# The scale of the exponentials from a ScalarE register in place of a per-partition operand

## The chip, the core and the metric

The kernel runs on one core of a Trainium2 chip. The core's engines have a queue each and run side by side: TensorE (PE in the profile; its weight loads are PEld), VectorE (DVE), ScalarE (ACT), GpSimd (POOL), and SyncE (SP), which here issues all the DMAs. The metric is the device time of the program in microseconds. The time before is 1566.49 us, the median of three runs (1566.06 to 1568.72).

## The reference

A transformer block whose attention and feed-forward parts both read the same normalised input (2048 rows of 512, 32 heads of 16, hidden width 1792, all float32):

```python
xn = _layernorm(x, axis=-1)
return x + _A_ref(xn, A_wqkv, A_wo) + _B_ref(xn, B_w1, B_b1, B_w2, B_b2)

# _A_ref, for 32 heads:
scores = jnp.einsum("bhqd,bhkd->bhqk", q, k) * (Dh ** -0.5)
p = _softmax(scores, axis=-1)
o = jnp.einsum("bhqk,bhkd->bhqd", p, v)
return (lambda x, *d: x.transpose(*d))(o, 0, 2, 1, 3).reshape(B, S, D) @ wo

# _B_ref:
h = jnp.einsum("bsd,df->bsf", x, w1) + b1
h = _gelu(h)                 # the tanh form
return jnp.einsum("bsf,fd->bsd", h, w2) + b2
```

## The kernel before

All matmuls of q, k, scores, output and feed-forward run on pairs of float16 halves (a high part and what is left), with weights scaled by powers of two. So the scores in PSUM are too large or small by a factor, which the softmax's exponential takes out: `sexp`, a tile of 128 partitions by 4 columns, holds that factor times 1/4, one column for each weight block of 128 columns, that is for two groups of four heads. All 128 partitions of a column hold the same value. DVE writes a column when it prepares that weight block (L463, L464), long before the first exponential that reads it, but for column 0.

Attention runs in units. There are 8 groups of four heads and 4 blocks of 512 queries, so 32 pairs; a pair has 16 units, 512 in all. In one unit, for each of four heads:

- `s_half` (L238 on) multiplies 128 queries by 512 keys into a PSUM bank `pS`, and DVE reduces it to row maxima, `mt` (L250). After 16 units the maxima of the pair are known, are negated (`mneg`, L261), split (`mhl`, L271 and L272) and written by DMA into two more rows of the query stack, so that the next product subtracts them.
- `e_half` (L284 on), 20 units later, multiplies 128 keys by 512 queries into a bank `pT`, and ACT takes the exponential of it into an SBUF tile `pe` (L295), with `scale=sexp[:, g // 2:g // 2 + 1]`. This is the instruction that the change touches; there are 2048 of it.
- `v_half` (L298 on), one or two units later, multiplies the exponentials by the values and a column of ones into `pV`; after 16 units ACT copies it out (`osb`, L321).

`unit` (L589 on) writes these in a fixed order: two score products, two exponential products, the value products on one half of TensorE's rows and, on the other half, some products of a filler (`pD`). The filler is first the projection of the next heads (ACT copies `pf`, L497), then the feed-forward part: DVE takes its hidden rows out of PSUM (`hh`, L996), GpSimd and ACT make the gelu (ACT's tanh, L963), and ACT takes out the sums (`yt`, L1022). TensorE's order is the written order (all queues are written out by hand, `ORDERED`), and most of its tiled products have one helper line, L169.

There are eight PSUM banks. The `pS` products turn through three, the `pT` products through three; one is the filler's `pD` (it and the `pT` banks change places when a filler group ends), and one holds `pV`. So a `pT` product waits until the exponential three before it has read its bank, and a `pS` product until the reduction three before it has. `given(engine, ns)` (L159) adds an estimate to a counter, which `unit` lowers; nothing reads it to set the order.

Of the kernel before, what the change touches and what calls it, by code (L numbers as in the profile page):

```python
# [10 lines left out]
I32 = mybir.dt.int32  # L11
AF = mybir.ActivationFunctionType
# [35 lines left out]
def layer_kernel(ctx: ExitStack, tc: tile.TileContext, x, wqkv, wo, w1, b1, w2, b2, out):  # L48
    nc = tc.nc
# [45 lines left out]
    sexp = const.tile([P, 4], F32, name="sexp")  # L95
# [11 lines left out]
    def banks(tag):  # L107
        k = free_banks[tag].pop(0)
        free_banks[tag].append(k)
        return bank_tile(k, tag)  # L110
# [48 lines left out]
    def given(engine, ns):  # L159
        backlog[engine] += ns  # L160
# [34 lines left out]
    def tiled(user, dst, lhs, rhs, start, stop):  # L195

        for j in range(0, P, 32):
            product(user, dst[j:j + 32], lhs[:, j:j + 32], rhs, start=start, stop=stop)


    mt_of, ptiles, pv_of = {}, {}, {}
    queue, slot = [], [0]

# [80 lines left out]
    def e_half(u, n):  # L284

        p, a = divmod(n, 2)
        t, kt = divmod(u, 16)
        g, qb = divmod(t, NQB)
        st = banks("T")
        r = slice(64 * a, 64 * a + 64)  # L290
        k0 = (kt % 4) * P
        tiled(None, st, kst[g % 2][p][kt // 4][r, k0:k0 + P], qst[g % 2][p][qb][r, :], True, True)
        pe = work.tile([P, QB], F32, name="pe", bufs=12)
        ptiles[u, n] = pe
        nc.scalar.activation(pe, st, AF.Exp, scale=sexp[:, g // 2:g // 2 + 1])  # L295
        given("act", 580)

    def v_half(u, a):  # L298

# [289 lines left out]
    def unit(gen):  # L589
# [7 lines left out]
        for a in range(2):  # L597
            for b in range(2 * a, 2 * a + 2):
                if u < NU:
                    s_half(u, b)  # L600
                if 0 <= e < NU:
                    e_half(e, b ^ 1)
            if e >= 0:
                enter()

                w, r = (e - 2, 1) if a == 0 else (e - 1, 0)
                live = 0 <= w < NU
                new = r == 0 and w % 16 == 0
                if live and not new:
                    v_half(w, r)  # L610
                dense(gen, 1 - r)
                if live and new:
                    v_half(w, r)

                for user, goes_on in (("V", live and not (r == 1 and w % 16 == 15)),
                                      ("D", cur[0] is not None and not cur[0].over())):
                    leave(user, goes_on)
                for k in backlog:
                    backlog[k] = max(0, backlog[k] - HALF)
                if live and r == 1:  # L620
                    v_end(w)
                ended()
# [559 lines left out]
```

## Time and profile before

| | us |
|---|---|
| median of the timed runs | 1566.49 |
| lowest and highest of them | 1566.06, 1568.72 |
| span of the profiled execution | 1563.9 |
| PE busy | 1521.8 |
| DVE busy | 1432.4 |
| ACT busy | 1376.1 |
| first and last exponential start | 128.4, 1530.9 |

The span goes from the first to the last instruction of one profiled execution; its own time is not listed beside it, so the timed median stands for it, 2.6 us above the span. A line such as L295 names an instruction of the kernel above. In a group of instructions, the count is followed by the busy time in us, the mean ns of one, the idle time of its engine just before them, and what ended that idle time. Busy times of one engine are unions, so overlapping neighbours are counted once. Ends of matmuls are modelled, and a few matmul records are missing. The granted clock of TensorE was 0.994 of full speed over the span.

### The profile page before, as it was taken

Reading aid. Unit: us, or ns where it says so; the run is one execution under the profiler, and the core shown is the slowest. Engines: PE = TensorE matmul, PEld = TensorE weight load, DVE = VectorE, ACT = ScalarE, POOL = GpSimd, SP = SyncE. Lnnn points to the kernel's source line nnn. Section 1 sums busy time; section 2 is a strip of 40 time slices with the busy share of each in tenths; the row PEclk is TensorE's granted clock in tenths of the full one; section 3 lists DMA queues with packets and bytes.
Section 4 is the critical chain, followed back from the end, with each engine's and each line's share of the span. In section 5 each row is a group of like instructions: output and inputs, shape, how many; then the busy total and the mean of one; then the engine's idle time right before and its main releaser. Section 6 shows DMA issues by size and latency. Waiting matters only on the chain.

```text
span 1563.9 us, 86366 instructions
## 1 busy us (share of the span) xinstructions
PE 1521.8 (97%) x39203; PEld 810.0 (52%) x39203; DVE 1432.4 (92%) x2428; ACT 1376.1 (88%) x2270; POOL 673.1 (43%) x694
## 2 busy tenths in 40 slices
PE   8999999999999999999999999999999999999997
PEld 4434555555555555555555555555555555555443
DVE  7889989999999999999999999999999999999612
ACT  4317999999999999999999999999999999999881
POOL 3113697446454444435443443654343454521000
PEclk9999999999999999999999999999999999999997
DMA  6454576442201211131122111121112111021512
GB/s 201 128 158 141 175 231 217 155 124 75 62 23 53 83 36 32 34 81 35 35 55 65 45 35 35 38 75 56 35 42 63 42 34 35 21 66 57 156 45 85
DMA packets 113672, 123.73 MB, mean 79 GB/s; under 512 B 24988, under 2 KB 85276, under 8 KB 113304
## 3 DMA queue, kind: packets, MB, share of 16 engines
q1 hardware_dynamic: 113304, 118.21, 25.6%
q8 instruction: 306, 5.01, 1.3%
q14 instruction: 62, 0.51, 0.1%
HBM read 80.61 MB, written 37.34 MB: 75 GB/s over the span
## 4 chain that ended last, share of the span: by engine, by line
PE 79%; DVE 14%; ACT 2%; DMA 2%; issue 2%; SPq 1%; POOL 0%; ACTq 0%; DVEq 0%; POOLq 0%
PE pV L169 23%; PE pS L169 19%; PE pD L169 18%; PE pT L169 15%; DVE mt L250 9%; DVE hh L996 3%; ACT pe L295 1%; PE pT L430 1%; PE pS L430 1%; DVE amx L658 1%; PE pT L523 1%; PE pD L430 1%; DMA ac<-acc_d 0%; PE pV L523 0%; SPq L1055 0%
## 5 line engine op out<-in xcount | busy, mean ns | idle before, releaser
L295 ACT ACTIVATE pe<-pT,sexp 128x512 f32<-128x512 f32 x2048 | 1267.7, 688 | 68.2 <-PE pS L169 21.3
L250 DVE TENSOR_REDUCE mt<-pS 128x1 f32<-128x512 f32 x2048 | 1291.7, 683 | 38.1 <-PE pS L169 20.3
L169 PE MATMUL pV<-pe,vv 64*32 64x512 f32 x8192 | 1076.6, 595 | 0.2
L169 PE MATMUL pT<-qst,kst 64*32 64x512 f16 x8192 | 712.8, 378 | 2.3 <-ACT pe L295 2.1
L169 PE MATMUL pS<-kst,qst 62*32 62x512 f16 x8192 | 638.8, 379 | 20.9 <-DVE mt L250 17.8
L169 PEld LDWEIGHTS <-qst 62*32 62x32 f16 x8192 | 277.3, 91 | 268.4 <-issue 114.4
L169 PEld LDWEIGHTS <-kst 64*32 64x32 f16 x8192 | 282.2, 91 | 177.0 <-issue 77.2
L169 PE MATMUL pD<-xb,wc 64*32 64x512 f16 x5376 | 370.5, 377 | 0.0
L169 PE MATMUL pD<-w_s,g 64*32 64x512 f16 x5376 | 359.4, 377 | 0.0
L169 PEld LDWEIGHTS pV<-pe,vv 64*32 64x32 f32 x8192 | 182.3, 105 | 106.3 <-PE pV L169 16.9
L974 POOL TENSOR_TENSOR t<-hh 128x512 f32<-128x512 f32 x56 | 58.2, 1039 | 350.0 <-DVE hh L996 350.0
L169 PEld LDWEIGHTS <-g 64*32 64x32 f16 x5376 | 115.1, 92 | 40.8 <-issue 0.4
L169 PEld LDWEIGHTS <-wc 64*32 64x32 f16 x5376 | 114.0, 91 | 35.9 <-issue 0.4
L169 PE MATMUL pD<-xt,wqk_h 64*32 64x512 f16 x1920 | 127.2, 378 | 1.7 <-issue 1.6
L351 POOL TENSOR_TENSOR osb<-osb,rb 128x512 f32<-128x512 f32 x31 | 39.8, 1285 | 131.6 <-DMA rb<-den_d 131.6
L1024 POOL TENSOR_TENSOR xa<-xa,yt 128x512 f32<-128x512 f32 x32 | 40.9, 1279 | 117.1 <-ACT yt L1022 117.1
L1061 DVE SCALAR_TENSOR_TENSOR ac<-pS,gs,ac 128x512 f32<-128x512 f32 x20 | 15.0, 751 | 67.2 <-PE pT L169 46.9
L969 POOL TENSOR_TENSOR t<-t,hh 128x512 f32<-128x512 f32 x56 | 71.6, 1279 | 4.7
L976 POOL TENSOR_TENSOR t<-t,hh 128x512 f32<-128x512 f32 x56 | 71.6, 1279 | 4.7
L971 POOL TENSOR_TENSOR g<-t,g 128x512 f16<-128x512 f32 x56 | 65.2, 1164 | 4.7
L968 POOL TENSOR_SCALAR t<-t,gs 128x512 f32<-128x512 f32 x56 | 38.8, 692 | 57.6 <-ACT t L963 57.6
L169 PE MATMUL pS<-wo_s,oc 64*32 64x512 f16 x1008 | 61.7, 378 | 0.3
(139 smaller groups left out, 880.5 us busy)
## 6 DMA issues: line engine op xcount, KB each, us to landing
wch<-in_B_w_dram SPq DMA_DIRECT2D x28, 512.0 KB
wc<-w_d SPq DMA_DIRECT2D x56, 256.0 KB
qk_d<-stg SPq DMA_DIRECT2D x32, 256.0 KB
rb<-den_d SPq DMA_DIRECT2D x124, 64.0 KB
w_d<-wsp SPq DMA_DIRECT2D x28, 256.0 KB
kst<-qk_d SPq DMA_DIRECT2D x128, 48.0 KB
qst<-qk_d SPq DMA_DIRECT2D x128, 48.0 KB
xs<-in_A_x_dram SPq DMA_DIRECT2D x16, 256.0 KB
```

The source lines that it names most:

```text
L169: p = nc.tensor.matmul(*args, **kw)
L250: nc.vector.reduce_max(mt_of[t][:, n, qt, kb:kb + 1], s, axis=AX.X)
L295: nc.scalar.activation(pe, st, AF.Exp, scale=sexp[:, g // 2:g // 2 + 1])
L351: pooled((1280, lambda: nc.gpsimd.tensor_tensor(osb, osb, rb, op=ALU.mult)), (620, lambda: nc.gpsimd.tensor_scalar(ot[:, 0], osb, 1.0, 0.0 ...
L430: nc.tensor.matmul(self.bank, lhs, rhs, start=start, stop=self.last and self.over())
L968: pooled((690, lambda: nc.gpsimd.tensor_scalar(t1, t1, 1.0, gs[:, 1:2], op0=ALU.add, op1=ALU.mult)), (1280, lambda: nc.gpsimd.tensor_tenso ...
L969: (1280, lambda: nc.gpsimd.tensor_tensor(t1, t1, hh, op=ALU.mult)),
L971: (1160, lambda: nc.gpsimd.tensor_tensor(g[:, 1, f, :], t1, g[:, 0, f, :], op=ALU.subtract)),
L974: pooled((1040, lambda: nc.gpsimd.tensor_tensor(t1, hh, hh, op=ALU.mult)), (620, lambda: nc.gpsimd.tensor_scalar(t1, t1, 1.0, 1.0 / GELU_A ...
L976: (1280, lambda: nc.gpsimd.tensor_tensor(t1, t1, hh, op=ALU.mult)),
L996: nc.vector.tensor_scalar(hh, hp, scale, bias, op0=ALU.mult, op1=ALU.add)
L1024: add = lambda: nc.gpsimd.tensor_tensor(xa, xa, yt, op=ALU.add)
```

## The change

The exponentials' scale is no longer an operand of 128 values in SBUF but a register of ScalarE. `exp_scale(m)` loads the register from partition 0 of column `m` of `sexp`, when `m` is another than the one it holds; since `m` is the group's number halved, that happens four times. The estimate of the exponential's time, 580 ns, becomes 470.

```diff
+    scale_reg, held = nc.scalar.alloc_register("exp_scale"), [None]
+
+    def exp_scale(m):
+
+        if held[0] != m:
+            nc.scalar.reg_load(scale_reg, sexp[0:1, m:m + 1].bitcast(I32))
+            held[0] = m
+        return scale_reg
+
     mt_of, ptiles, pv_of = {}, {}, {}
     queue, slot = [], [0]
...
-        nc.scalar.activation(pe, st, AF.Exp, scale=sexp[:, g // 2:g // 2 + 1])
-        given("act", 580)
+        nc.scalar.activation(pe, st, AF.Exp, scale=exp_scale(g // 2))
+        given("act", 470)
```

New lines shift those below: L295 before is L304 in the changed kernel, L1022 is L1031, L963 is L972. On ScalarE the first load stands ahead of the table load and the first exponentials, behind the copies of the projection. After the change:

```order
L506 ACTIVATE pf<-pT 128x512 x3
L506 ACTIVATE pf<-pD 128x512
L206 TENSOR_LOAD sexp
L304 ACT_TABLE_LOAD
L304 ACTIVATE pe<-pT 128x512 x4
```

One row is new there, and the exponentials no longer name `sexp`. The second load stands where the third group of four heads begins, between two sets of four exponentials. Before (a tanh, then eight exponentials, a copy `yt`, two more, and the copy `osb`):

```order
L963 ACTIVATE t_13381<-t_13381 128x512
L295 ACTIVATE pe<-pT,sexp 128x512 x8
L1022 ACTIVATE yt<-pD,gs 128x512
L295 ACTIVATE pe<-pT,sexp 128x512 x2
L321 ACTIVATE osb<-pV 128x512
```

After:

```order
L972 ACTIVATE t_13382<-t_13382 128x512
L304 ACTIVATE pe<-pT 128x512 x4
L206 TENSOR_LOAD sexp
L304 ACTIVATE pe<-pT 128x512 x4
L1031 ACTIVATE yt<-pD,gs 128x512
L304 ACTIVATE pe<-pT 128x512 x2
L330 ACTIVATE osb<-pV 128x512
```

The third and fourth load stand in the same way at the fifth and seventh group. On all other engines the rows and their order are the same but for the line numbers.

## Prediction

> **What bounds the kernel now.** I read the busy shares and the chain of waits on the page first.
>
> ```profile
> PE 1521.8 (97%) x39203; PEld 810.0 (52%) x39203; DVE 1432.4 (92%) x2428; ACT 1376.1 (88%) x2270; POOL 673.1 (43%) x694
> PE 79%; DVE 14%; ACT 2%; DMA 2%; issue 2%; SPq 1%; POOL 0%; ACTq 0%; DVEq 0%; POOLq 0%
> ```
>
> ACT, whose instructions the change makes cheaper, has 2% of the chain. Taken alone this says that the change is worth nothing. The shares are averages over stages, so the next view is the table of stretches, with the attention loop (first exponentials to the last score products) in one stretch:
>
> ```profile
> 180.49:1436.72 1256.23, 1239.02 (x34400) 678.52 (x34403) 1222.81 (x2022) 1200.99 (x1982) 612.41 (x603) 1.00 0.23 66
> 400.00:1400.00 1000.00, 988.02 (x27419) 541.21 (x27410) 980.52 (x1622) 958.16 (x1582) 452.58 (x456) 1.00 0.17 46
> 656.00:664.00 8.00, 8.00 (x248) 4.42 (x248) 7.92 (x14) 7.55 (x13) 4.37 (x5) 1.00 0.02 5
> 664.00:672.00 8.00, 7.84 (x220) 4.46 (x205) 7.41 (x12) 8.00 (x15) 4.27 (x5) 1.00 0.33 86
> ```
>
> The columns are PE, weight loads, DVE, ACT and POOL, busy us and instruction count. Three engines are nearly full: in the 1000 us from 400 on, PE is idle 12.0, DVE 19.5 and ACT 41.8 us. So none has room for long, and each can hold the others for a moment. The last two rows show such a moment. From 664 to 672 ACT is busy for all of the 8.00 us; PE starts 220 matmuls against 248 in the 8 us before, although it is called busy for 7.84 us; DVE falls from 7.92 to 7.41 us. PE's busy time does not tell its pace. What ACT did there:
>
> ```profile
> 665.10 0.60 ACT L321 ACTIVATE osb<-pV 128x512 f32<-128x512 f32 x1
> 665.58 1.28 ACT L295 ACTIVATE pe<-pT,sexp 128x512 f32<-128x512 f32 x2
> 666.72 0.66 ACT L963 ACTIVATE t<-t 128x512 f32<-128x512 f32 x1
> 667.24 2.45 ACT L295 ACTIVATE pe<-pT,sexp 128x512 f32<-128x512 f32 x4
> 669.51 0.75 ACT L1022 ACTIVATE yt<-pD,gs 128x512 f32<-128x512 f32 x1
> 670.09 3.14 ACT L295 ACTIVATE pe<-pT,sexp 128x512 f32<-128x512 f32 x5
> 669.56 2.56 DVE L250 TENSOR_REDUCE mt<-pS 128x1 f32<-128x512 f32 x4 [0.42 <-PE pS L169]
> ```
>
> Three instructions that are no exponentials come within 4.4 us, ACT runs without a gap, and DVE then waits 0.42 us for a score product. PE takes its instructions in order: a pT product that waits for a pT bank, which an exponential has not yet read out, holds the pS products behind it, for which DVE waits. This is where ACT sets the end: not in the plain units, but for a unit or two after each extra instruction.
>
> **The price of the operand.** The groups of ACT by form:
>
> ```profile
> L295 ACT ACTIVATE pe<-pT,sexp 128x512 f32<-128x512 f32 x2048 | 1267.7, 688 | 68.2 <-PE pS L169 21.3 <-PE pT L169 19.1 <-ACT pe L295 0.2
> L963 ACT ACTIVATE t<-t 128x512 f32<-128x512 f32 x56 | 35.6, 636 | 0.0
> L1022 ACT ACTIVATE yt<-pD,gs 128x512 f32<-128x512 f32 x32 | 22.2, 695 | 0.0
> L497 ACT ACTIVATE pf<-pD 128x512 f32<-128x512 f32 x21 | 12.6, 598 | 6.0 <-PE pS L126 3.6 <-PE pD L169 1.5 <-PE pS L169 0.5
> L713 ACT ACTIVATE xs<-xs,sd 128x512 f32<-128x512 f32 x6 | 4.0, 714 | 0.2
> ```
>
> L1022 and L497 are the same copy from PSUM, with and without a scale that is read from a tile: 695 against 598 ns, 97 ns. The exponential, 688 ns, reads such a scale too (sexp among its names). L963 multiplies by a constant scale and reads no scale tile: 636 ns from SBUF, against 714 for L713, which reads one: 78 ns. So the cost is the reading of the operand and not the multiplication. I take 97, from the pair that reads PSUM like the exponential does: it becomes 591 ns. What counts is the distance between starts, since neighbours overlap. In the rows above, four exponentials in a row take 2.45 us, so they start (2.45 - 0.69)/3 = 0.587 us apart; after L321, which reads no operand, the next starts 665.58 - 665.10 = 0.48 us later. So the distance falls by 0.10 us, to about 0.49. In the loop that is 1848 exponentials times 0.10 = 185 us of ACT's time.
>
> ```profile
> L295 ACT ACTIVATE pe<-pT,sexp 128x512 f32<-128x512 f32 x1848 | 1143.0, 688 | 53.1 <-PE pS L169 19.0 <-PE pT L169 8.9 <-ACT pe L295 0.2
> L250 DVE TENSOR_REDUCE mt<-pS 128x1 f32<-128x512 f32 x1848 | 1165.6, 683 | 30.7 <-PE pS L169 14.0 <-PE pT L169 3.9 <-PE pD L169 1.3
> ```
>
> Nearly all of it becomes idle time. 1848/4 = 462 units in 1256.23 us make 2.72 us for a unit of four exponentials. They need 4 x 0.587 = 2.35 us now and 4 x 0.49 = 1.96 us then. An extra instruction of about 0.5 us now overruns its unit by 2.35 + 0.5 - 2.72 = 0.13 us and takes the next unit's room as well; then it fits into its own unit with 0.26 us left.
>
> **What of it reaches the end.** DVE's reductions stay as they are, and no matmul is removed. So the gain is at most the time in which DVE waits in this loop: 1256.23 - 1222.81 = 33.4 us. The part that can go is where its reductions wait for PE for long enough to be named, by the view of waits for 400 to 1400, and then for 180 to 400:
>
> ```profile
> DVE mt L250 <- PE pS L169: 8.2, 31, 0.4
> DVE mt L250 <- PE pT L169: 0.9, 4, 0.3
> ...
> DVE mt L250 <- PE pS L169: 5.1, 10, 1.5
> DVE mt L250 <- PE pT L169: 3.0, 8, 0.6
> ```
>
> The 9.1 us of the first stretch I count as gone: 35 waits of 0.26 us on average, the size of a unit's overrun and of the one shown at 669.56. The other gaps before the reductions there are short ones in plain units, where the products themselves come late; they stay. Of the 8.1 us of 180 to 400 I count half, 4: up to 1.5 us long, they also have loads and weight preparation behind them, and no row divides them. Before 180 and after 1437 I count nothing: the first exponentials come at 128, and in the tail there are no reductions and ACT is busy 119.00 of 136.00 us:
>
> ```profile
> 1400.00:1536.00 136.00, 134.74 (x3587) 69.10 (x3580) 78.52 (x130) 119.00 (x194) 12.99 (x12) 1.00 0.27 83
> ```
>
> Gain: 9.1 + 4 = 13.1 us, bounds 0 and 33.4.
>
> **The four loads.** Each stands in ACT's own queue, ahead of an exponential: one ahead of the table load and the first exponential, three at the change of head pairs in mid-loop. They wait only for a sexp value that DVE wrote one quarter of the heads earlier, so for nothing. Behind each stand the exponentials, and behind those PE's next pT product. The trace has no register load. The nearest rows of ACT are
>
> ```profile
> L295 ACTq EVENT_SEMAPHORE  x509: 17/17/1093, 137.0 to 1529.0; - x170
> L295 ACT ACT_TABLE_LOAD  x1: 1283/1283/1283, 127.1 to 127.1; - x1
> ```
>
> 17 ns for a queue instruction that finds its value there, 1283 ns for one that brings in state. I take the middle, 0.65 us, for want of a nearer row, and let all four reach the end: 2.6 us, bounds 0.1 and 5.1. If a unit's slack hid them, the result would be 2.6 us better.
>
> The Trainium skill, "DMA: Bandwidth & Descriptors", section "Latency and other measured facts", puts the floor of a tensor load at about 600 ns; by it the four would cost 2.4 us and the sum below would be 0.2 us lower. No run here shows it yet.
>
> The estimate at L304 (470 for 580) only adds to a counter that nothing reads for the order. All other engines keep their rows, so it costs nothing and needs no cover.
>
> **Sum.** Against the profiled span: 1563.9 - 13.1 + 2.6 = 1553.4 us. The timed median, 1566.49, lies 2.6 us above that span; I keep this distance: 1556 us.
>
> **The rivals.**
> *PE is the bound after all.* For it: PE's 79% of the chain, and that PE names waits for exponentials for only 2.1 us in all:
>
> ```profile
> PE pT L169 <- ACT pe L295: 2.1, 7, 0.7
> ```
>
> Then 2.1 us are gained and 2.6 paid: 1567 us. Against it stand 220 matmuls against 248 in equal busy time. The Trainium skill, "Perfetto Trace Analysis", section "Identifying the Most-Contended Engine", says that matmul busy time is a poor measure of how near PE is to its limit, and to look at weight-load busy time. By that rule PE, with 52% of weight loads, would have room; the trace agrees as far as the matmul counts go.
>
> *All of DVE's waiting goes.* DVE then runs without a gap: 1566.5 - 33.4 + 2.6 = 1536 us. For it: ACT would be idle some 20% of the loop. Against: the plain units wait for products too.
>
> *The register does not count as a constant.* The exponential stays at 688 ns: only the loads are left, 1566.5 + 2.6 = 1569 us. Against it speaks L963, whose scale costs nothing; but its constant stands in the instruction, and a register is not seen anywhere in this trace.
>
> *Slower: the register is fetched at each instruction, and neighbours no longer overlap.* Exponentials would start 0.688 us apart. With the loop's other ACT work, 1200.99 - 1143.0 = 58 us, ACT would need 1848 x 0.688 + 58 = 1329 us for a loop of 1256: 73 us more, 1642 us with the loads. It decides from a distance of (1256 - 58)/1848 = 0.648 us on, 0.06 above today's. For it: each of the 1848 would need the register. Against: no row shows that ACT's queue is late; it names only PE as what its idle exponentials wait for.
>
> **How the numbers follow.** The forecast has 0.65, PE as bound 0.13, all of DVE's waiting 0.11, an unchanged exponential 0.06, lost overlap 0.05. The range for 8 in 10 goes from 1543 (a gain of 26 us of the 33.4, loads nearly free) to 1567 (PE as bound). A measurement of this kernel tells about 0.2%, 3.1 us, from no change; faster than 1563.4 are the forecast and the full gain, and none of the others: 0.76. Within 0.2% falls PE as bound, with a part of the unchanged exponential: 0.15. Slower: 0.09.
>
> **What would show it.** Exponentials of 585 to 600 ns, about 0.49 us apart in the rows of x4; L1022 unchanged at 695. ACT's busy time in the loop down by about 185 us, to some 81% of it. The named waits of DVE's reductions from 400 to 1400 down from 9.1 to under 2 us, DVE over 99% busy there. Gaps of 0.1 to 1.3 us on ACT at the four loads. I am wrong in the step on what reaches the end if the exponentials shrink and the span does not; in the price if they stay at 688; in the loads if the gaps there reach several us.

## The result and the profile after

The changed kernel takes 1558.35 us, the median of 7 runs (1554.96 to 1560.89); before it is 1566.49 us in 7 runs of the same comparison (1563.89 to 1571.85). The ratio is 0.9942, with a 95% interval of 0.9927 to 0.9958: 0.58% faster, some 9 us of 1566. The medians alone lie 8.1 us apart. The profiled span goes from 1563.9 to 1557.1 us.

The page of the changed kernel, with the busy shares and the chain:

```profile
PE 1513.2 (97%) x39203; PEld 808.8 (52%) x39203; DVE 1429.9 (92%) x2428; ACT 1221.3 (78%) x2270; POOL 674.7 (43%) x694
PE 80%; DVE 15%; issue 2%; DMA 1%; SPq 1%; ACT 0%; POOL 0%; DVEq 0%; ACTq 0%; POOLq 0%
```

ACT lost 154.8 us of busy time and the span lost 6.8. ACT's 2% of the chain are gone. Its groups by form, and the exponentials' neighbours:

```profile
L304 ACT ACTIVATE pe<-pT 128x512 f32<-128x512 f32 x2048 | 1109.8, 597 | 208.8 <-PE pS L169 99.3 <-PE pT L169 79.2
L1031 ACT ACTIVATE yt<-pD,gs 128x512 f32<-128x512 f32 x32 | 22.0, 688 | 3.6 <-PE pT L169 0.3 <-PE pS L169 0.2
```

An exponential takes 597 ns instead of 688, as long as the copies without an operand (593 to 605). The other forms stay: the copy with an operand is at 688 ns for 695, tanh at 636 for 636. ACT's idle time before exponentials rises from 68.2 to 208.8 us: the shorter exponentials mostly wait longer for their products. The stretches of the loop, in the columns of the table before:

```profile
180.49:1430.00 1249.51, 1229.56 (x34344) 676.17 (x34336) 1218.77 (x2018) 1059.82 (x1976) 611.54 (x601) 1.00 0.23 66
400.00:1400.00 1000.00, 988.54 (x27616) 544.24 (x27612) 986.29 (x1633) 855.77 (x1595) 455.37 (x458) 1.00 0.17 47
```

From 400 to 1400 DVE is now busy for 986.29 us instead of 980.52, and does 1633 instructions instead of 1622. ACT has 144 us to spare. What DVE's reductions still wait for there, and the group with all its idle time:

```profile
DVE mt L259 <- PE pS L169: 3.5, 18, 0.5
...
L259 DVE TENSOR_REDUCE mt<-pS 128x1 f32<-128x512 f32 x1492 | 939.0, 682 | 11.7 <-PE pS L169 3.5
```

The named waits fell from 9.1 to 3.5 us, the whole idle time before the reductions from 17.4 to 11.7 us, and 1492 reductions fit into the 1000 us instead of 1481, 0.74% more.

The same copy, tanh and four exponentials that stood without a gap before stand like this now:

```profile
663.28 1.08 ACT L304 ACTIVATE pe<-pT 128x512 f32<-128x512 f32 x2 [0.29 <-PE pT L169]
664.25 0.60 ACT L330 ACTIVATE osb<-pV 128x512 f32<-128x512 f32 x1
664.74 1.09 ACT L304 ACTIVATE pe<-pT 128x512 f32<-128x512 f32 x2
665.70 0.65 ACT L972 ACTIVATE t<-t 128x512 f32<-128x512 f32 x1
666.22 2.09 ACT L304 ACTIVATE pe<-pT 128x512 f32<-128x512 f32 x4
653.08 15.35 DVE L259 TENSOR_REDUCE mt<-pS 128x1 f32<-128x512 f32 x24
```

ACT waits 0.29 us for a product before the two exponentials ahead of the copy, so it comes to the extra instructions with nothing left over. DVE runs 24 reductions in a row, to 668.43, without a named wait.

The four loads are in the trace too (first the view of their line, then ACT's rows around the second, at 487.6):

```profile
L206 ACTq TENSOR_LOAD <-sexp x4: 274/280/887, 125.1 to 1174.9; - x4
...
486.27 2.19 ACT L304 ACTIVATE pe<-pT 128x512 f32<-128x512 f32 x4
```

The three loads in the loop take 274 to 283 ns. The second falls inside a set of four exponentials: it starts 0.24 us after the third of them, and the fourth starts 0.49 us after the third, the usual distance. The load goes on in the queue while the exponential ahead of it is still under way.

### The profile page after: what moved, and what is told of

Same layout as the page of the kernel before. It is cut to its first block, busy times and chain, and to the rows that moved or that the text cites. A ratio compares the mean times of both kernels' runs of the same rounds, so it can differ in the third digit from the quotient of the medians.

```text
span 1557.1 us, 86371 instructions
## 1 busy us (share of the span) xinstructions
PE 1513.2 (97%) x39203; PEld 808.8 (52%) x39203; DVE 1429.9 (92%) x2428; ACT 1221.3 (78%) x2270; POOL 674.7 (43%) x694
## 4 chain that ended last, share of the span: by engine, by line
PE 80%; DVE 15%; issue 2%; DMA 1%; SPq 1%; ACT 0%; POOL 0%; DVEq 0%; ACTq 0%; POOLq 0%
PE pV L169 24%; PE pS L169 19%; PE pD L169 18%; PE pT L169 15%; DVE mt L259 10%; DVE hh L1005 3%; PE pT L439 1%; PE pS L439 1%; DVE amx L667 1%; PE pT L532 1%; PE pV L532 0%; SPq L1064 0%; DMA ac<-acc_d 0%; PE pD L439 0%; DMA qk_d<-stg 0%
## 5 line engine op out<-in xcount | busy, mean ns | idle before, releaser
L304 ACT ACTIVATE pe<-pT 128x512 f32<-128x512 f32 x2048 | 1109.8, 597 | 208.8 <-PE pS L169 99.3
L169 PEld LDWEIGHTS <-qst 62*32 62x32 f16 x8192 | 280.9, 91 | 268.9 <-issue 112.0
L169 PEld LDWEIGHTS <-kst 64*32 64x32 f16 x8192 | 267.0, 91 | 166.4 <-issue 68.0
```

Of the source, the lines that this page charges most:

```text
L169: p = nc.tensor.matmul(*args, **kw)
L304: nc.scalar.activation(pe, st, AF.Exp, scale=exp_scale(g // 2))
```

## The experiments

The ratio is against the kernel before, timed beside each of them (its medians there are 1565.62 to 1566.82 us). The last column is a number that startup differences do not touch: the time from the start of the 257th to that of the 1793rd exponential (384 units) in the profiled execution. It comes from one execution each. Kernels that should agree in it do so within 0.5 us: 1038.4 and 1038.9 with the operand, 1030.7 to 1030.9 with a register or a constant. Below, "in the loop" means this number.

| kernel | median us | ratio and 95% interval | 257th to 1793rd, us |
|---|---|---|---|
| before | 1566.49 | 1 | 1038.4 |
| changed (register) | 1558.35 | 0.9942 (0.9927 to 0.9958) | 1030.8 |
| const_scale | 1556.91 | 0.9937 (0.9923 to 0.9950) | 1030.9 |
| loads_only | 1567.14 | 1.0005 (0.9993 to 1.0016) | 1038.9 |
| half_register | 1559.32 | 0.9952 (0.9938 to 0.9965) | 1032.6 |
| load_each_unit | 1557.78 | 0.9939 (0.9925 to 0.9953) | 1030.7 |
| operand_no_tanh | 1564.42 | 0.9982 (0.9972 to 0.9991) | 1035.7 |
| register_no_tanh | 1558.70 | 0.9954 (0.9938 to 0.9970) | 1031.8 |
| register_hh_act | 1556.48 | 0.9938 (0.9925 to 0.9951) | 1027.8 |
| operand_hh_act | 1573.00 | 1.0036 (1.0022 to 1.0051) | 1043.9 |
| register_late_bank | 1577.96 | 1.0067 (1.0048 to 1.0086) | 1042.9 |
| register_mid_bank | 1559.99 | 0.9956 (0.9940 to 0.9972) | 1031.6 |
| reg_late_bank_hh_act | 1596.56 | 1.0192 (1.0172 to 1.0211) | 1063.1 |
| two_operands | 1624.05 | 1.0369 (1.0350 to 1.0387) | 1088.5 |

### The register and the loads by themselves

A constant in place of the register:

```diff
-        nc.scalar.activation(pe, st, AF.Exp, scale=exp_scale(g // 2))
+        nc.scalar.activation(pe, st, AF.Exp, scale=2.0 ** -8)
```

> The scale is the constant 2^-8 written into the instruction (the value that these inputs give for every head; the four loads are gone). Theory (a register costs an exponential nothing more than a constant, and the four loads are hidden): exponentials of 597 ns as with the register, and the time within 2 us of the register form, 1556 to 1560 us. Rival (the register still costs something at each instruction, or the loads reach the end with the 2.6 us of the prediction): 2.5 us or more faster than the register form, under 1556 us.

Measured: 1556.91 us, 1.4 us under the register form, with intervals that overlap; in the loop 1030.9 against 1030.8 us. Its exponentials are as long as with the register:

```profile
L304 ACT ACTIVATE pe<-pT 128x512 f32<-128x512 f32 x2048 | 1109.8, 597 | 206.1 <-PE pS L169 109.4 <-PE pT L169 76.6
```

A register costs no more than a constant that could be measured here, and the four loads, which this run lacks, do not show either.

The loads without their use:

```diff
-        nc.scalar.activation(pe, st, AF.Exp, scale=exp_scale(g // 2))
+        exp_scale(g // 2)
+        nc.scalar.activation(pe, st, AF.Exp, scale=sexp[:, g // 2:g // 2 + 1])
```

> The four register loads stay, but the exponentials take their scale from the tile again. Theory (a load of 0.28 us runs beside the exponential that is already under way): same as before, 1565 to 1568 us, exponentials 688 ns. Rival (each load reaches the end): with the 0.65 us of the prediction each, 2.6 us slower, 1569 us.

Measured: 1567.14 us, the same as before. But the trace has no load: at its line it shows four waits of 17 ns, presumably because nothing reads the register. So this run says only that the four waits are free. The loads themselves are tried by loading the register for each unit:

```diff
-        if held[0] != m:
+        if held[0] != u:
...
-        nc.scalar.activation(pe, st, AF.Exp, scale=exp_scale(g // 2))
+        nc.scalar.activation(pe, st, AF.Exp, scale=exp_scale(u, g // 2))
```

> The register is loaded anew for each unit, 512 loads in place of 4. Theory (a load is hidden behind the exponential under way or the wait for the next product): within 3 us of the register form, 1557 to 1561 us. Rival (a load holds up ACT's queue for its whole 0.28 us, and that is no longer free when it comes in each unit): ACT needs 4 x 0.49 + 0.28 = 2.24 us of a unit, so still less than before, but an extra instruction overruns again: 1561 to 1566 us. If each load reached the end in full: 512 x 0.28 = 143 us more, 1700 us.

Measured: 1557.78 us, and 1030.7 us in the loop. 512 loads cost no more than 4:

```profile
L206 ACTq TENSOR_LOAD <-sexp x512: 272/277/1386, 127.9 to 1519.4; - x171
```

The loads take 154 us together and none of it appears. In the trace all 512 begin while an ACT instruction is still under way, and 505 of them end beside one too; the other seven end in ACT's wait for the next product.

### How much of the shortening is needed

Half of the exponentials with the register, half with the operand:

```diff
-        nc.scalar.activation(pe, st, AF.Exp, scale=exp_scale(g // 2))
+        nc.scalar.activation(pe, st, AF.Exp, scale=exp_scale(g // 2) if n < 2 else sexp[:, g // 2:g // 2 + 1])
```

> Two of the four exponentials of a unit take the register, two the tile. ACT needs 2 x 0.49 + 2 x 0.587 = 2.15 us of a unit of 2.72, so an extra instruction of 0.5 us still fits into its own unit. Theory A (the gain is that an extra instruction no longer overruns its unit, and is used up once it fits): three quarters or more of the gain, 1558 to 1560.5 us. Theory B (every exponential that frees its bank sooner gives its own share): half of the gain, about 1562.5 us.

Measured: 0.9952 against 0.9942; in the loop 5.8 of 7.6 us, three quarters of the gain for half of the shortening. That is theory A's number. The intervals of the two ratios overlap, and half of the gain (0.9971) lies outside this one's, 0.9938 to 0.9965.

The edit in the other direction, a second operand for each exponential in the kernel before:

```diff
+    zero = const.tile([P, 1], F32, name="zero")
+    nc.gpsimd.memset(zero, 0.0)
...
-        nc.scalar.activation(pe, st, AF.Exp, scale=sexp[:, g // 2:g // 2 + 1])
+        nc.scalar.activation(pe, st, AF.Exp, scale=sexp[:, g // 2:g // 2 + 1], bias=zero)
```

> The kernel before with a second operand per partition on each exponential, a bias tile of zeros: the edit in the other direction. By 0.10 us for an operand the distance between exponentials goes from 0.587 to 0.69 us. Theory (ACT's load against a unit's room has a knee: free below, in full above): ACT needs 1848 x 0.69 + 58 = 1333 us for a loop of 1256, so 60 to 100 us slower than before, 1625 to 1665 us. Rival (the time goes with the exponential's duration evenly, 9 us for 0.09 us): 9 us slower, 1575 us. Second rival (a bias tile costs nothing beside a scale tile): 1565 to 1568 us.

Measured: 1624.05 us, 3.7% slower, just under the range. ACT is full. The last two rows are the pair of exponentials between the copy `osb` and the tanh, the same two that the prediction (at 665.58) and the section on the result (at 664.74) show:

```profile
400.00:1400.00 1000.00, 991.42 (x26063) 538.26 (x26055) 940.74 (x1548) 998.42 (x1509) 439.22 (x443) 1.00 0.16 44
L297 ACT ACTIVATE pe<-pT,zero,sexp 128x512 f32<-128x512 f32 x2048 | 1411.4, 895 | 8.4 <-PE pT L171 4.6 <-PE pS L171 2.4
685.55 1.58 ACT L297 ACTIVATE pe<-pT,zero,sexp 128x512 f32<-128x512 f32 x2
686.88 0.77 ACT L965 ACTIVATE t<-t 128x512 f32<-128x512 f32 x1
```

So one operand more costs 58 us and one less gains 9. The price of an operand is the same both times. From the first of these two exponentials to the tanh it is 0.96 us without an operand, 1.14 with one and 1.33 with two, that is 0.48, 0.57 and 0.665 us for each. Over 400 to 1400 us the usual distance from an exponential to a tanh right behind it is 0.477, 0.569 and 0.663 us: 92 and 94 ns for an operand. The mean duration, 895 ns, would have put the second at 207. The kernel before stood just below the knee: of a unit of some 2.7 us, four exponentials back to back take 4 x 0.569 = 2.28 us there and 4 x 0.663 = 2.65 us here, where any extra instruction runs over.

### Where the gain arises

The 56 tanh instructions of ACT are left out, so that the gelu has none, in the kernel before and in the changed one:

```diff
             def tanh():
-                nc.scalar.activation(t1, t1, AF.Tanh, scale=GELU_C * GELU_A)
-                given("act", 600)
                 later(1, rest, True)
```

> The kernel before without its 56 tanh instructions on ACT (the gelu is then without its tanh; all else stands). Theory A (ACT sets the end only in the units behind an extra instruction of its own; tanh are 56 of 116 extras in the loop): about half of the register's gain of 8 us appears already, 1561 to 1564 us. Theory B (each exponential counts by itself): nothing or up to 1 us, 1565 to 1567 us.

> The changed kernel without its 56 tanh instructions. Theory A: with the register a tanh fits into its unit, so taking it away gives little: 1556 to 1559 us, 0 to 2 us under the register form; and against the kernel before without tanh the register gives only some 4 us. Theory B: the register's whole gain of 8 us stands between the two kernels without tanh.

Measured: without tanh the kernel before is 0.18% faster (0.09 to 0.28), 2.7 us in the loop, a little less than expected. The changed kernel has no gain from it: 0.9954 against 0.9942, and the loop is 1.0 us longer, not shorter, for a reason that stays open. So between the two kernels without tanh the register gains 0.9954/0.9982, 0.28%, in the loop 4.0 us, where it gains 7.6 with tanh. About half of the gain belonged to the units with a tanh, as theory A has it; theory B would have left all of it.

The traces also tell in which units the time was saved. ACT's order shows which of the 384 units have one of its 105 extra instructions (tanh, `osb`, `yt`) among or just ahead of their four exponentials. I took the length of each unit from the reductions (first reduction of one unit to first of the next, for the scores that are written beside these exponentials), and set the kernel before against the changed kernel and against the half register:

| extra instructions in the unit and the one before it | units | saved by the register, us | saved by the half register, us |
|---|---|---|---|
| none | 196 | 0.35 | 0.21 |
| one | 166 | 3.68 | 3.10 |
| two or more | 22 | 3.58 | 2.49 |

Units with no extra instruction near them gain next to nothing, although their exponentials are shortened like all others: that is theory A and not B. Nearly half of the gain lies in 22 units, 0.16 us in each, where two extra instructions come close together. A single one is worth 0.02 us in each of the two units near it. The run with the constant repeats the division: 0.21, 3.71 and 3.58 us.

To see who held PE, I set the start of each pT, pS and first pD product from 320 to 1340 us against the recorded end of the ACT or DVE instruction that it waits for in the program, and counted those that start within 0.13 us of it, that is, those which were held:

| held by | before | changed | half register | register, no tanh | register, hh on ACT | late bank |
|---|---|---|---|---|---|---|
| pT by an exponential | 208 | 91 | 99 | 70 | 156 | 176 |
| first pD of a group by an exponential | 68 | 4 | 68 | 0 | 6 | 4 |
| pS by a reduction | 161 | 168 | 166 | 167 | 57 | 166 |
| pT by hh | 43 | 43 | 43 | 43 | 43 | 0 |

The change took away 117 of 208 waits for exponentials at pT, and half of it 109. These are counts, not times: without tanh the kernel before still has 200 of them, and is 2.7 us shorter in the loop. Those at the first pD went with the change and not with half of it, though that has three quarters of the gain: they are worth little. The view of waits of before named 7 of them in the whole span, 2.1 us; the others lie beside matmuls on the other half of the rows, so that PE was called busy.

### What sets the end now

If it were DVE's fullness, taking hh off DVE should help:

```diff
-                nc.vector.tensor_scalar(hh, hp, scale, bias, op0=ALU.mult, op1=ALU.add)
+                nc.scalar.activation(hh, hp, AF.Identity, scale=scale, bias=bias)
```

> The changed kernel with the 56 hh instructions (scale and bias of the hidden rows, 0.72 us each on DVE) moved to ACT. Theory (with the register DVE is what fills the loop, 986 of 1000 us, and ACT has room, 856 of 1000): DVE loses 56 x 0.72 = 40 us of work, and half or more of it reaches the end: 1525 to 1540 us. Rival (PE's own order sets the pace): within 4 us of the register form, 1554 to 1562 us.

> The same move of hh to ACT in the kernel before, where ACT is 96% full in the loop: it gets 56 instructions of about 0.6 us more, 33 us in 1256 us, that is 98%. Theory (ACT then sets the end): much less gain than with the register, 1550 to 1564 us. Rival (ACT's load does not matter): the same gain as with the register, 26 to 41 us.

Measured: with the register nothing that can be told from the changed kernel (0.9938 against 0.9942; in the loop of one execution 3.0 us less), so the theory of a full DVE fell. The time is the one that its rival gave, but that PE's own order sets the pace is not shown by it. With the operand it is 0.36% slower than before. Both have the same move; the register makes a difference of 16.5 us here instead of 8.1. The loop of the first, and its wait:

```profile
400.00:1400.00 1000.00, 992.57 (x27756) 547.16 (x27747) 965.43 (x1591) 884.89 (x1650) 454.09 (x457) 1.00 0.17 47
DVE mt L259 <- PE pS L169: 23.4, 65, 0.8
PE pT L169 <- ACT pe L304: 6.2, 16, 0.4
```

DVE is free for 35 us and waits for PE; neither DVE nor ACT is full. The table above suggests why: 43 of the hh in the middle of the loop end just before the pT product that takes their bank, on whichever engine they run.

So the next theory, C, was that bank. A finished filler group gives its bank to the pT products; the first pT behind the start of the next group takes it, while hh still reads it. The late bank moves it behind the two other pT banks, the mid bank behind one of them:

```diff
+    freed = [None]
+
     def hold(tag, other):
         k = free_banks[tag if free_banks[tag] else other].pop(0)
+        if tag == "D" and free_banks["T"] and free_banks["T"][0] == freed[0]:
+            free_banks["T"].append(free_banks["T"].pop(0))
...
                 free_banks["T"].append(self.key)
+                freed[0] = self.key
```

This is the late bank; the mid bank has `free_banks["T"].insert(1, free_banks["T"].pop(0))` in the line below the `if`. The third run has the late bank and hh on ACT.

> The changed kernel with another order of the pT banks: the bank that a finished filler group has freed is taken by the third pT product after the new group has begun, and no longer by the first. Theory C (what holds PE at each hh is that the next pT product takes the bank that hh is still reading; 43 of some 53 hh in the middle of the loop end 0.05 us before that product starts, on DVE as on ACT): the wait of up to 0.7 us goes, and the two pT banks that are left turn faster, which costs some 0.1 to 0.3 us each time: 5 to 20 us under the register form, 1538 to 1553 us. Rival (DVE's 0.72 us of work for hh delay the reductions and with them the pS products in any case): within 4 us of the register form, 1554 to 1562 us; or slower, if two banks are too few.

> As the late bank, but the freed bank is taken by the second pT product, 0.2 us later than in the changed kernel. Theory C: a gain of 0.2 us for some 50 of 56 hh, about 8 to 10 us under the register form, 1547 to 1551 us. Rival (DVE's work for hh sets the wait): within 3 us of the register form.

> The late bank together with hh on ACT. Theory C: moving hh to ACT gave nothing because the bank's next user waited for it there too; without that wait, DVE's 40 us less of work come through: 15 to 35 us under the register form, 1523 to 1543 us. Rival: the pT products now wait for exponentials that stand behind hh on ACT: no better than the late bank with hh on DVE.

Measured: the waits for hh vanish (43 to 0 with both banks) and nothing is gained. The mid bank is as fast as the changed kernel (0.9956), the late bank 20 us slower than it, and with hh on ACT 38 us. More pT products wait for exponentials instead, 134 with the mid bank, 176 with the late bank and 212 with hh on ACT too, where the changed kernel has 91. That fits the third case expected, "two banks are too few": while hh holds its bank, the pT products turn on two. Theory C named a true wait, but the cure moves it. What sets the pace of the plain units now is not shown by these runs, and what one more PSUM bank would give stays open; all eight are in use. No version tried is measurably faster than the changed kernel by the timed runs.

## Why the prediction was right

The forecast was 1556 us (1543 to 1567); 1558.35 came. By its steps:

- **The price of the operand** held: 597 ns for the forecast 591, and 0.49 us between starts (two in a row take 1.09 us, the second of them 0.60). The pair of copies with and without an operand, 97 ns apart, was the right row for it; the exponential fell by 91, and its usual distance by 92.
- **ACT's load** was oversized in its effect: 185 us less busy time in the loop were forecast, 1200.99 - 1059.82 = 141 came. Exponentials that wait for a product no longer overlap with the one ahead (from 400 to 1400 us, 1120 start beside the exponential ahead of them before, and 771 after), so busy time falls by less than the distance between starts.
- **What reaches the end in mid-loop**: of the 9.1 us of named waits from 400 to 1400, 5.6 went, not "under 2 us" left but 3.5, and DVE came to 98.6%, not over 99%. In time it is 7.6 us in the 1038.4 between the two exponentials, 7.3 us per 1000. The term was right in kind and a quarter too large. The mechanism, an extra instruction that overruns its unit, is borne out by the runs with half of the shortening and without tanh, and by the units: all but 0.35 of the 7.6 us lie beside extra instructions. But the overrun of 0.13 us, worked out for a single one, was too large: what the register saved beside a single one is 0.02 us in each of the two units near it, and it takes two close together, as in the moment that the prediction shows, for 0.16.
- **The 4 us of 180 to 400** did not come. From the first to the 257th exponential, which covers most of that stretch, it takes 186.6 us before, and 189.1, 184.8 and 185.0 in the changed kernel, with the constant and with a load for each unit; they differ among themselves by as much as the term. Nothing can be said for it.
- **The loads** cost nothing, where 2.6 us were forecast. "Let all four reach the end" was the failed step: a load runs beside work in hand. It took away most of what the 4 us that did not come had added, so it is partly luck that the sum came out nearer than its terms: 10.5 us of gain were forecast, and 8.1 came between the medians.
- **The rivals**: that PE names only 2.1 us of waits for exponentials did not mean that it had only these. The register does count as a constant. The knee of the slower rival is real: it put it at a distance of 0.648 us, and the run with a second operand, at 0.663 us and more, is 58 us slower than the kernel before. What would have brought it about did not happen: the neighbours overlap as before.
- **Two readings** were wrong and changed nothing. "In the tail there are no reductions": 51 of the 2048 start after 1436.72 us, the last at 1471.9, with 1.0 us of named waits; from the 1793rd exponential to the end it takes 210.5 us before and 209.7 after. And the lower bound of 1543 us is 1566.5 - 26 + 2.6, so it pays for the loads in full, where the text calls them nearly free.

## What to carry to other kernels

When three engines run a loop at 96 to 99%, price a shorter instruction by the units in which its engine overruns, not by its count: here 1848 x 0.092 = 170 us of spacing were worth 9, and 22 units in 384 gave nearly half of what the loop gained. A scale that is the same on all partitions belongs in a register or a constant on ScalarE, which saved 91 ns for each instruction here and cost nothing that could be measured. Before work is moved off the fullest engine, look at which bank the next product takes: the 43 waits for hh stayed when hh went to ACT, though no run shows that they alone kept the gain away.

## What was not expected of the hardware

A register load in ScalarE's queue took 0.27 to 0.28 us in the loop, and 512 of them added nothing. The Trainium skill, "DMA: Bandwidth & Descriptors", section "Latency and other measured facts", gives a floor of about 600 ns for a tensor load; the loads of this case, from SBUF, are under half of that, so for them the measurement decides. The operand's 91 ns agree with the 93 ns that the Trainium skill, "ScalarE: Activation LUTs", section "What ACT_TABLE_LOAD costs", gives. A second operand cost as much again, but only the distance between starts shows it: 0.477, 0.569 and 0.663 us with none, one and two. The mean duration went to 895 ns with ACT full, 207 ns more, and the copy `yt` from 695 to 875 without any edit. On a full ScalarE the distance between starts is what to read, and not the duration.
